# Soft-MoE attention kernel: the last batch's turns one step sooner, the last sigmoid in two parts, other PSUM places for the kept logits and the last batch's tiles

## The chip, the cores and the metric

One NeuronCore of a Trainium2 chip runs the whole program. The metric is the device time of one execution in microseconds (us). Three runs of the kernel before gave 369.21, 370.83 and 370.82 us: the median is 370.82 us.

## What is computed

Attention with a sigmoid in place of a softmax, and a soft mixture of experts on its output. Cut to what matters:

```python
B, H, S, D = 8, 12, 448, 64                      # q, k, v: float32
scores = q @ k.transpose(0, 1, 3, 2) / sqrt(D) - log(S)
x = (sigmoid(scores) @ v) -> (B * S, H * D)       # 3584 tokens x 768
logits = x @ phi                                  # 32 slots: 8 experts x 4
d = softmax(logits, over the tokens)              # dispatch
slot_out[e] = relu((d.T @ x)[e] @ w1[e]) @ w2[e]  # w1: 8 x 768 x 1024, w2: 8 x 1024 x 768
out = softmax(logits, over the slots) @ slot_out  # combine, 3584 x 768
```

## The kernel before, in words

Everything is float32. Heads are worked on in pairs: 8 batches of 6 pairs are 48 pairs. A pair's keys come in three full chunks of 128; the last 64 keys of two neighbouring pairs share a fourth. So two pairs take seven steps, `seq` has 168 of them, and a step is one `score` (L271: four products into a PSUM tile `sc`), one sigmoid over 128x896 on ScalarE (L290) and one `weigh` (L300: products with V into the `av` banks). From step 156 on a `weigh` comes one step after its `score`. `evac_a` (ScalarE) and `evac_b` (VectorE, L330) add a pair's `av` banks up into `x`. Pair 47 is cut into two parts of 256 and 192 queries in two banks (`weigh_half`, L295), with `evac_last` (L332) on VectorE.

TensorE, SyncE (SP), VectorE and ScalarE run in the order in which the code is written. **GpSimd's order alone is chosen by the scheduler** (`MANUAL`, L65, leaves it out). Waits are put in by the framework, which follows each tile as a whole: two PSUM banks that were allotted as one tile count as one.

*Turns.* The slot products need `x` with tokens on the partitions. VectorE turns it by 32x32 blocks (`turns`, L341, into a queue `todo`, which `work` empties at a pace set for each step). The last batch's turns of pairs 42 to 44 (`x` in `wpx`, turned into `wpy`) are put into the queue at steps 158 and 159 (L586, L587).

*The softmax over tokens* runs on as groups of batches end. At step 161 `slot_job` (L461) multiplies the group before the last by its weights; VectorE takes the result out of a `sc` tile (L471), which the next `score` needs. GpSimd's `old_rows` (L449) brings that sum back as rows of the last group.

*After the last step* `last_job` (L489) ends the softmax. TensorE makes the logits of pairs 45 and 46 (L497) and of 47 (L498), turns `x` of the three pairs (`turn_pe`, L356, twelve products into `px`) and does two products `warm` into `pw`, whose values nobody reads. VectorE then adds the logits and takes their maximum (L504); VectorE, GpSimd and ScalarE each move one quarter of it (L506) for a maximum over all (L507), and of the result (L509); ScalarE takes the exponentials (L512), VectorE turns them (L514), and TensorE makes the slots: `slot_mm` of `k1=1` into `pw` (L530) and of the rest into the tile of the logits (L531). VectorE turns these into `phi` (`turn_slots`, L527) and `w1` begins (L187). GpSimd also runs `old_rows` and a memset (L510, L511) for the slots of the last three pairs, which overwrite part of that `x`.

*Where things lie.* `lgt` and `pxt` are two `sc` tiles of two banks each, bank 0 and bank 1. In the kernel before bank 0 of `lgt` holds the last logits and bank 0 of `pxt` the turned pair 47; the bank 1s hold the logits of the earlier groups, copied there by `keep` (L596) for the combine softmax, since their place `ltile` is then loaded with weights (`load_kept`, L125). `pw` and `px[0]` are the `av` banks `av00` and `av01`.

*Weights.* `w1` and `w2` (50 MB) stream through a ring of tiles; SP issues all loads in the order of the code, and each waits until the tile's last reader is done. Behind the last step come loads into `big` (L169), `lt` (L127), `wpy` (which needs the products of L530 and L531 done), then three into `wa`, each for one quarter tile that the first `w1` products (L187) have read, and then whole `wa` tiles as `w1` goes on. Outputs are stored by the same queue at the end (L787, L794, L801).

## Time and profile before

| | us |
|---|---|
| median of three runs | 370.82 |
| the profiled execution, its own time | 370.77 |
| its span, from the first to the last instruction | 369.0 |
| TensorE busy (4341 matmuls) | 348.9 |
| VectorE busy | 242.5 |
| ScalarE busy | 222.3 |
| GpSimd busy | 10.1 |

The profile is of one execution; 1.77 us of its time lie outside the span. Times in the rows are us from the span's start. Attention runs to about 277.6, `last_job` to 283.9 and `w2` to 342.6; the outputs end at 369. PE is TensorE's matmuls, PEld its weight loads, DVE VectorE, ACT ScalarE, POOL GpSimd and SPq the issuing of DMAs by SP. The ends of matmuls are modelled by the profiler.

### The profile page before, as it was taken

To read this page: it belongs to the slowest core of one execution; us is meant where nothing else is said; L and a number is where in the kernel's file an instruction comes from. 1 tells how busy PE (TensorE), PEld (TensorE's weight loads), DVE (VectorE), ACT (ScalarE), POOL (GpSimd) and SP (SyncE) were. 2 spreads that over 40 slices of the span, in tenths; PEclk is the share of its full clock that TensorE was granted. 3 is DMA by queue.
4 is the path that set the end of the run, shared out by engine and by line. 5 is a ranking of instruction groups with operands and counts; after the bars stand their busy time and mean duration, and the time that the engine had idled before them with its cause. 6 is when DMAs were issued, how large, how long until landed. Compare 5 with 4: busy or idle time off the path is not lost.

```text
span 369.0 us, 10403 instructions
## 1 busy us (share of the span) xinstructions
PE 348.9 (95%) x4341; PEld 175.3 (48%) x4341; DVE 242.5 (66%) x621; ACT 222.3 (60%) x307; POOL 10.1 (3%) x45
## 2 busy tenths in 40 slices
PE   8999999999999999999999999999999999699850
PEld 5666666634444455444344644463446553233630
DVE  0158829796894986769859695978856785124650
ACT  5777777577777765777777387757573114323640
POOL 1000000000000000000000000010103001000000
PEclk9999999999999999999999999999999999979995
DMA  7666666465576663766667387739989999999998
GB/s 219 229 216 213 187 213 219 140 216 177 203 228 220 203 204 93 223 216 199 192 211 229 95 282 257 254 92 351 330 299 317 413 435 431 412 424 402 375 412 292
DMA packets 34927, 95.21 MB, mean 258 GB/s; under 512 B 3648, under 2 KB 17600, under 8 KB 33472
## 3 DMA queue, kind: packets, MB, share of 16 engines
q1 hardware_dynamic: 34880, 94.55, 72.8%
q8 instruction: 34, 0.56, 0.6%
q14 instruction: 13, 0.11, 0.1%
HBM read 83.53 MB, written 11.01 MB: 256 GB/s over the span
## 4 chain that ended last, share of the span: by engine, by line
PE 83%; DMA 8%; DVE 3%; ACT 1%; issue 1%; ACTq 0%; DVEq 0%
PE sc L281 34%; PE av L323 33%; DMA wa<-in_w_dram 7%; PE av L834 3%; PE av L187 3%; PE sc L445 2%; PE sc L383 2%; PE av L780 2%; DVE wpy L347 1%; DVE wa L781 1%; PE pt L780 1%; DMA wk<-in_qk_dram 1%; PE av L298 1%; PE av L818 1%; PE sc L365 1%; PE sc L762 1%
## 5 line engine op out<-in xcount | busy, mean ns | idle before, releaser
L290 ACT ACTIVATE big<-sc,sm 128x896 f32<-128x896 f32 x167 | 167.7, 1007 | 78.4 <-PE sc L281 75.3
L323 PE MATMUL av<-big 64*64 64x448 f32 x1292 | 163.3, 536 | 0.1
L281 PE MATMUL sc<-big 64*64 64x448 f32 x896 | 119.9, 537 | 0.4 <-DVE xy L471 0.4
L323 PEld LDWEIGHTS av<-big 64*64 64x64 f32 x1292 | 59.9, 133 | 65.3 <-issue 51.0
L281 PEld LDWEIGHTS sc<-big 64*64 64x64 f32 x896 | 42.6, 133 | 44.5 <-issue 29.3
L281 PE MATMUL sc<-wk 64*64 64x448 f32 x440 | 62.3, 538 | 0.1
L347 DVE STREAM_TRANSPOSE wa<-wpe 32x384 f32<-32x384 f32 (+5 forms) x144 | 58.0, 403 | 2.2
L347 DVE STREAM_TRANSPOSE wa<-xy 32x192 f32<-32x192 f32 (+3 forms) x96 | 33.1, 344 | 1.6
L330 DVE TENSOR_TENSOR wpe<-wpe,av 128x448 f32<-128x448 f32 x18 | 11.2, 621 | 31.5 <-PE av L323 20.3
L281 PEld LDWEIGHTS sc<-wk 64*64 64x64 f32 x440 | 21.6, 134 | 21.3 <-issue 14.5
L347 DVE STREAM_TRANSPOSE wa<-wpx 32x288 f32<-32x288 f32 (+1 forms) x48 | 24.9, 519 | 0.8
L834 PE MATMUL av<-wa,hw 128*32 128x384 f32 x208 | 21.8, 521 | 2.9 <-DMA wa<-in_w_dram 2.9
L330 DVE TENSOR_TENSOR wpx<-wpx,av 128x448 f32<-128x448 f32 x15 | 9.3, 621 | 19.8 <-PE av L323 17.5
L187 PE MATMUL av<-wa,phi 128*32 128x256 f32 x312 | 17.6, 380 | 0.4 <-DVE phi L527 0.4
L781 DVE COPY wa<-pt 128x384 f32<-128x384 f32 x23 | 11.8, 555 | 3.2 <-PE pt L780 2.8
L330 DVE TENSOR_TENSOR xy<-xy,av 128x448 f32<-128x448 f32 x14 | 8.7, 621 | 7.6 <-ACT xy L326 5.9
L781 ACT COPY wa<-av 128x384 f32<-128x384 f32 x23 | 10.6, 479 | 4.7 <-PE av L780 4.1
L187 PEld LDWEIGHTS av<-wa,phi 128*32 128x32 f32 x312 | 9.6, 110 | 7.3 <-DVE tmp L724 0.9
L727 ACT COPY t<-tmp 128x32 f32<-128x32 f32 x8 | 1.7, 218 | 17.5 <-DVE tmp L725 13.6
L771 ACT CAST big<-sc 128x512 fp32r<-128x512 f32 (+5 forms) x11 | 4.4, 432 | 11.5 <-PE sc L762 11.5
L347 DVE STREAM_TRANSPOSE wpe<-xy 32x256 f32<-32x256 f32 (+3 forms) x32 | 11.0, 344 | 0.5
L834 PEld LDWEIGHTS av<-wa,hw 128*32 128x32 f32 x208 | 5.1, 111 | 10.3 <-issue 4.7
(189 smaller groups left out, 285.0 us busy)
## 6 DMA issues: line engine op xcount, KB each, us to landing
wa<-in_w_dram SPq DMA_DIRECT2D x52, 384.0 KB, 4.0
big<-in_qk_dram SPq DMA_DIRECT2D x32, 448.0 KB, 3.6
wa<-in_wq_dram SPq DMA_DIRECT2D x6, 1536.0 KB, 30.7
wa<-in_w_dram SPq DMA_DIRECT2D x3, 3072.0 KB, 22.3
big<-in_v_dram SPq DMA_DIRECT2D x46, 192.0 KB, 2.5
wk<-in_qk_dram SPq DMA_DIRECT2D x15, 448.0 KB, 3.4
out_dram<-wa SPq DMA_DIRECT2D x13, 384.0 KB, 7.3
out_dram<-wa SPq DMA_DIRECT2D x2, 1536.0 KB, 7.4
```

Source lines behind the costliest of these rows:

```text
L187: nc.tensor.matmul(ph[32 * j:32 * j + 32, 0:256], phi_sb[:, kc, :], wt, start=(kc == 0), stop=(kc == NKC - 1))
L281: nc.tensor.matmul(sc[h][64 * t:64 * t + 64, 0:S], qkts[pt][r, S + k0:S + k0 + 64], qkts[pt][r, 0:S], start=True, stop=True)
L290: nc.scalar.activation(att, tile2[:, :, 0:S], AF.Sigmoid, bias=nbias, scale=QSCALE)
L323: nc.tensor.matmul(o[t][r, 0:S], w, att[row, h, :], start=start, stop=stop)
L330: nc.vector.tensor_tensor(out=x_of(p), in0=x_of(p), in1=av[0][:, 0:S], op=ALU.add)
L347: nc.vector.transpose(y[32 * g:32 * g + 32, k0:k0 + n, c0:c0 + m, BLK * a:BLK * a + BLK], src)
L383: nc.tensor.matmul(lg[32 * j:32 * j + 32, BLK * c0[j]:BLK * (c0[j] + n)], phi_sb[:, hp, :], blocks(x, j if x is xa else (j + 2) % 4, n), s ...
L445: nc.tensor.matmul(sls[t][32 * a:32 * a + 32, BLK * k0:BLK * k1], zt[:, c * BLK:(c + 1) * BLK], y_of(t, gi, c)[:, k0:k1, BLK * a:BLK * a + ...
L771: nc.scalar.copy(cts[i][:, m:m + w], pt[:, at0 - t0:at0 - t0 + w])
L780: nc.tensor.matmul(pf[:, 0:HALF], ct_of(m, t, n), sts[hf], start=True, stop=True)
L781: (nc.scalar.copy, nc.vector.tensor_copy)[k % 2](ov, pf[:, 0:HALF])
L834: nc.tensor.matmul(po[32 * fl:32 * fl + 32, 0:HALF], h[:, k:k + NSLOT], w2_chunk(hf, e, g, fl), start=(n == 0), stop=(n == 2 * E - 1))
```

## The change

- The last batch's turns of pairs 42 and 43 go into the queue at step 157 and are worked off there, the rest at step 158 (`LAST_T`, and a pace that begins one step sooner). `last_v` stays in step 158.
- The last sigmoid is cut into the two parts of queries (128x512 and 128x384 elements). The logits of pairs 45 and 46 stand ahead of the last product with V in TensorE's order.
- The kept logits of both halves are copied in the last step, into pair 46's banks (`av00`, `av01`). The bank 1s of `lgt` and `pxt` become `pw` and `px[0]`, and the `w1` products use them until `state["kept"]` is cleared. `load_kept` moves up by one place among the loads.

```diff
+LAST_T = 8
@@ score
+            elif u == seq[-1]:
+                flat = att.rearrange("p h s -> p (h s)")
+                att = [flat[:, 2 * t.start:2 * t.stop].rearrange("p (h s) -> p h s", h=2) for t in parts]
+                for k, t in enumerate(parts):
+                    nc.scalar.activation(att[k], tile2[:, :, t], AF.Sigmoid, bias=nbias, scale=QSCALE)
@@ last_job
             evac_last(p)
-            logits(lg, b, range(TR, NPR - 1), first=TR)
@@ the table of steps
-        late[u + SLOT_AT] += [lambda: turns(B - 1, 0, 0, 2, 0, EARLY), lambda: work(B * S)]
-        late[u + SLOT_AT + 1] = [lambda: turns(B - 1, 0, 2, 1, 0, EARLY), lambda: turns(B - 1, 0, 0, 3, EARLY)]
+        del late[u + SLOT_AT]
+        late[u + LAST_T] = [lambda: work(B * S), lambda: turns(B - 1, 0, 0, 2, 0, EARLY), lambda: work(B * S)]
+        late[u + LAST_T + 1] = [lambda: turns(B - 1, 0, 2, 1, 0, EARLY), lambda: turns(B - 1, 0, 0, 3, EARLY)]
-        for i in range(u + 10, u + 31):
+        for i in range(u + 9, u + 31):
@@ keep
-            nc.vector.tensor_copy(t[:, 1, 0:w], lts[i][:, 0:w])
+            nc.vector.tensor_copy(t[:, 0:w], lts[i][:, 0:w])
@@ the loop over the steps
                 if i == len(seq) - 1:
+                    kept = [ps_av.tile([P, 512], F32, name=f"av0{t}") for t in range(2)]
+                    keep(1, kept[1])
                     lgt = ps_sc.tile([P, 2, 512], F32, name="sc")
-                    keep(1, lgt)
+                    keep(0, kept[0])
                     logits_old(lgt[:, 0, :])
             else:
-                nc.scalar.activation(dmx[0:1, :], atts[seq[-1]][0:1, 0, 0:1], AF.Exp)
+                logits(lgt[:, 0, 0:P], B - 1, range(TR, NPR - 1), first=TR)
+                nc.scalar.activation(dmx[0:1, :], atts[seq[-1]][1][0:1, 0, 0:1], AF.Exp)
@@ after the loop
-        pw = ps_av.tile([P, 512], F32, name="av00")
-        px = [ps_av.tile([P, 512], F32, name="av01")]
         pxt = ps_sc.tile([P, 2, 512], F32, name="sc")
-        keep(0, pxt)
-        px += [pxt[:, 0, :], ps_av.tile([P, 512], F32, name="av10")]
+        pw, px = lgt[:, 1, :], [pxt[:, 1, :], pxt[:, 0, :], ps_av.tile([P, 512], F32, name="av10")]
@@ av_tile
+        if name == "av0" and state["kept"]:
+            return (lgt, pxt)[turn[name] % 2][:, 1, :]
...
-        if k == 6:
+        if k == 5:
             load_kept()
```

How it moves instructions, at three places. Engines' waits stand in brackets.

VectorE at steps 157 to 161, before: L330 adds up pair 44, L347 are the turns, L471 takes the slots out of their `sc` tile.

```order
L330 TENSOR_TENSOR wpx_72<-wpx_72,av00_2788 128x448 [waits PE_49,Activation_49]
L347 STREAM_TRANSPOSE wpy_73<-wpx_72 32x2x4x32 [waits DVE_49]
L347 STREAM_TRANSPOSE wpy_73<-wpx_72 32x2x4x32 x5
L347 STREAM_TRANSPOSE wpy_73<-wpx_72 32x4x32 [waits DVE_49]
L347 STREAM_TRANSPOSE wpy_73<-wpx_72 32x4x32 x5
L347 STREAM_TRANSPOSE wpy_73<-wpx_72 32x3x4x32 x2
L476 MEMSET t1_2660 64x32
L471 SCALAR_TENSOR_TENSOR xy_89<-xy_89,t1_2660,sc_2878 128x3x32 [waits PE_49]
L471 SCALAR_TENSOR_TENSOR xy_89<-xy_89,t1_2660,sc_2878 128x3x32
L347 STREAM_TRANSPOSE wpy_73<-wpx_72 32x3x3x32 x8
```

The same place now (L337, L354 and L478 are what L330, L347 and L471 were):

```order
L354 STREAM_TRANSPOSE wpy_73<-wpx_72 32x2x4x32 [waits DVE_49]
L354 STREAM_TRANSPOSE wpy_73<-wpx_72 32x2x4x32 x5
L337 TENSOR_TENSOR wpx_72<-wpx_72,av00_2788 128x448 [waits PE_49,Activation_49]
L354 STREAM_TRANSPOSE wpy_73<-wpx_72 32x4x32 [waits DVE_49]
L354 STREAM_TRANSPOSE wpy_73<-wpx_72 32x4x32 x5
L354 STREAM_TRANSPOSE wpy_73<-wpx_72 32x3x4x32 x2
L354 STREAM_TRANSPOSE wpy_73<-wpx_72 32x3x3x32 x3
L483 MEMSET t1_2660 64x32
L478 SCALAR_TENSOR_TENSOR xy_89<-xy_89,t1_2660,sc_2881 128x3x32 [waits PE_49]
L478 SCALAR_TENSOR_TENSOR xy_89<-xy_89,t1_2660,sc_2881 128x3x32
L354 STREAM_TRANSPOSE wpy_73<-wpx_72 32x3x3x32 x5
```

Six turns moved ahead of the addition, and three more ahead of the row that empties the slots' tile.

GpSimd (POOL) after the last step, before: the copies to `sm` are its quarters of the maximum, those to `xy` are `old_rows`.

```order
L451 COPY xy<-xy 32x3x32 [waits DVE_49,Pool_49]
L506 COPY sm<-sm 32x1 [waits DVE_49]
L509 COPY sm<-sm 32x1 [waits DVE_49]
L451 COPY xy<-xy 32x3x32 [waits PE_49]
L451 COPY xy<-xy 32x3x32
L511 MEMSET xy 32x3x128 [waits Pool_49]
```

And now:

```order
L458 COPY xy<-xy 32x3x32 [waits DVE_49,PE_49]
L458 COPY xy<-xy 32x3x32
L517 MEMSET xy 32x3x128 [waits Pool_49]
L512 COPY sm<-sm 32x1 [waits DVE_49]
L515 COPY sm<-sm 32x1 [waits DVE_49]
```

The two copies of `old_rows`, which wait for TensorE's last turn of `x`, and the memset moved ahead of the quarters of the maximum.

TensorE over the same stretch, before: L298 is the end of the last product with V, L365 the logits, L359 the turns, L339 `warm`, L445 the slots; a buffer's number tells its tile.

```order
L298 MATMUL av11_2981<-big_75,xy_89 64x192 x2
L365 MATMUL sc_3005<-xy_89,phi_69 32x96 [waits DVE_49,PE_49]
...
L365 MATMUL sc_3005<-xy_89,phi_69 32x64 [waits DVE_49]
...
L365 MATMUL sc_3005<-xy_89,phi_69 32x32 x2
L359 MATMUL av01_3021<-csb_66,xy_89 128x128 x3
...
L359 MATMUL av10_3024<-csb_66,xy_89 64x128
L339 MATMUL av00_3020<-csb_66 128x128 x2
L445 MATMUL av00_3020<-wpy_73,t1_2660 32x32 [waits DVE_49]
L445 MATMUL av00_3020<-wpy_73,t1_2660 32x32 x11
L445 MATMUL av00_3020<-wpy_73,t1_2660 32x32 [waits Pool_49] x4
L445 MATMUL sc_3005<-wpy_73,t1_2660 32x64 x16
```

And now (L305, L372, L366, L346 and L452 are what L298, L365, L359, L339 and L445 were):

```order
L372 MATMUL sc_3009<-xy_89,phi_69 32x128 x2
L305 MATMUL av10_2980<-big_75,xy_89 64x256 [waits Activation_49]
L305 MATMUL av10_2980<-big_75,xy_89 64x256
L305 MATMUL av11_2981<-big_75,xy_89 64x192 [waits Activation_49]
L305 MATMUL av11_2981<-big_75,xy_89 64x192
L372 MATMUL sc_3009<-xy_89,phi_69 32x64 [waits DVE_49]
...
L366 MATMUL av10_3033<-csb_66,xy_89 64x128
L346 MATMUL sc_3009<-csb_66 128x128 x2
L452 MATMUL sc_3009<-wpy_73,t1_2660 32x32 [waits DVE_49]
L452 MATMUL sc_3009<-wpy_73,t1_2660 32x32 x11
L452 MATMUL sc_3009<-wpy_73,t1_2660 32x32 [waits Pool_49] x4
L452 MATMUL sc_3009<-wpy_73,t1_2660 32x64 x16
```

The logits of two pairs moved ahead of the last V, and `warm` and the first slots, which went to a bank of their own (`av00_3020`), now go to the tile that holds the logits (`sc_3009`).

VectorE's readers of these tiles, before:

```order
L504 ISA t1_2660,sm_67<-sc_3005,t1_2660 128x128 [waits DVE_49,PE_49]
...
L527 STREAM_TRANSPOSE phi_69<-av00_3020 128x32 [waits DMAHW6_49,PE_49]
L485 COPY xy_89<-av01_3021 128x128 [waits Activation_49]
L527 STREAM_TRANSPOSE phi_69<-sc_3005 128x64 [waits PE_49]
L487 COPY xy_89<-sc_3022 64x128 [waits Pool_49]
L487 COPY xy_89<-av10_3024 64x128
```

And now:

```order
L510 ISA t1_2660,sm_67<-sc_3009,t1_2660 128x128 [waits DVE_49,PE_49]
...
L533 STREAM_TRANSPOSE phi_69<-sc_3009 128x32 [waits DMAHW6_49,PE_49]
L492 COPY xy_89<-sc_3032 128x128 [waits Activation_49]
L533 STREAM_TRANSPOSE phi_69<-sc_3009 128x64
L494 COPY xy_89<-sc_3032 64x128
L494 COPY xy_89<-av10_3033 64x128
```

The rows stand in the same order and read other tiles. Of the two turns of the slots only the first still waits for TensorE. In the built program the count for which L504 waited was that of the last logits' product; L510's is that of the second `warm` product. The count for the first turn of the slots (L527, now L533) was that of the last 32x32 product and is now that of the last 32x64 product.

## Rows read from the trace of the kernel before

**Rows 1.** Busy time by stretch: window, length, engines, granted clock, DMA share, GB/s

```profile
280.00:285.00 5.00, 4.50 (x143) 2.99 (x146) 3.20 (x14) 1.44 (x7) 2.02 (x7) 1.00 0.86 310
285.00:290.00 5.00, 5.00 (x91) 2.93 (x87) 3.50 (x14) 0.45 (x2) 0.85 (x4) 1.00 1.03 390
```

**Rows 2.** Chain of waits in time order: start, us, what

```profile
287.02 7.95 PE av L187 x144
294.99 27.03 DMA wa<-in_w_dram
322.06 1.51 PE av L834 x8
```

**Rows 3.** Timeline of SP's issues: start, us, queue, line, DMA

```profile
281.45 0.33 SPq L169 DMA_DIRECT2D wpy<-in_w_dram  x1
282.04 1.78 SPq L165 DMA_DIRECT2D wa<-in_wq_dram  x3
285.47 1.62 SPq L169 DMA_DIRECT2D wa<-in_wq_dram  x2
```

**Rows 4.** Timeline at steps 158 to 162: start, us, engine, line [idle before <-releaser]

```profile
259.55 0.62 DVE L330 TENSOR_TENSOR wpx<-wpx,av 128x448 f32<-128x448 f32 x1 [1.79 <-PE av L323]
...
266.53 3.86 DVE L347 STREAM_TRANSPOSE wpy<-wpx 32x288 f32<-32x288 f32 x8
...
266.64 0.98 PE L281 MATMUL sc<-big 64*64 64x448 f32 x8 [0.41 <-DVE xy L471]
```

**Rows 5.** Timeline, end of attention

```profile
274.80 0.53 DVE L598 COPY sc<-lt 128x352 f32<-128x352 f32 x1 [1.20 <-ACT big L290]
...
275.59 1.01 ACT L290 ACTIVATE big<-sc,sm 128x896 f32<-128x896 f32 x1 [0.82 <-PE sc L281]
...
276.65 0.98 PE L298 MATMUL av<-big,xy 128*64 128x256 f32 x8 [0.28 <-ACT big L290]
...
277.56 0.87 PE L365 MATMUL sc<-xy,phi 128*32 128x96 f32 x32
```

**Rows 6.** Timeline, from the maximum to the first products with w1

```profile
278.51 0.29 DVE L504 CUSTOM_DVE_ANT_0 t<-sc,t 128x128 f32<-128x128 f32 x1 [0.45 <-PE sc L365]
...
278.87 0.18 POOL L506 COPY sm<-sm 32x1 f32<-32x1 f32 x1 [11.01 <-DVE sm L504]
...
279.18 0.14 DVE L507 TENSOR_REDUCE sm<-sm 32x1 f32<-32x4 f32 x1 [0.19 <-ACT sm L506]
279.29 0.60 PE L359 MATMUL av<-csb,xy 128*128 128x128 f32 x4
...
279.72 0.61 PE L339 MATMUL av<-csb 128*128 128x128 f32 x4
...
279.95 0.56 POOL L451 COPY xy<-xy 32x96 f32<-32x96 f32 x2 [0.38 <-PE av L359]
...
280.43 0.46 PE L445 MATMUL av<-wpy,t 128*32 128x32 f32 x32
...
280.57 0.41 POOL L511 MEMSET xy<- 32x384 f32 x1
...
280.70 0.68 PE L445 MATMUL sc<-wpy,t 128*32 128x64 f32 x32
...
281.07 0.22 DVE L527 STREAM_TRANSPOSE phi<-av 128x32 f32<-128x32 f32 x1 [0.18 <-PE av L445]
...
281.34 1.50 PE L187 MATMUL av<-wa,phi 128*32 128x256 f32 x24
281.42 0.25 DVE L527 STREAM_TRANSPOSE phi<-sc 128x64 f32<-128x64 f32 x1
```

**Rows 7.** Busy time by half us where TensorE last stood still

```profile
319.00:319.50 0.50, 0.34 (x3) 0.10 (x1) 0.32 (x2) 0.06 (x1) 0.00 (x0) 1.00 0.87 369
...
321.00:321.50 0.50, 0.00 (x0) 0.00 (x0) 0.00 (x0) 0.00 (x0) 0.00 (x0) 0.92 0.99 393
...
328.00:328.50 0.50, 0.50 (x5) 0.15 (x3) 0.00 (x0) 0.00 (x0) 0.00 (x0) 0.76 0.99 418
```

More of the change, by code (lines that the diff above doesn't have):

```diff
@@ L97, in soft_moe_attention @@
     N_SEQ = len(units) - 2
-    state = {"next": 0, "ring": 0, "used": 0, "room": 0, "n8": 0, "call": 0}
+    state = {"next": 0, "ring": 0, "used": 0, "room": 0, "n8": 0, "call": 0, "kept": True}
     utile, quads = {}, {}
@@ L296, in weigh_half @@
             for k, t in enumerate(parts):
+                a = att[k] if isinstance(att, list) else att[:, :, t]
                 for h, r in enumerate(heads):
-                    nc.tensor.matmul(o[k][r, 0:t.stop - t.start], w[:, r], att[:, h, t], start=start, stop=stop)
+                    nc.tensor.matmul(o[k][r, 0:t.stop - t.start], w[:, r], a[:, h, :], start=start, stop=stop)
         def weigh(u):
@@ L597, in keep @@
             n, w = 0, LTW[i]
-            nc.vector.tensor_copy(t[:, 1, 0:w], lts[i][:, 0:w])
+            nc.vector.tensor_copy(t[:, 0:w], lts[i][:, 0:w])
             for gi in range(2 * i, 2 * i + 2 + i):
                 wd = (lt_at + [lt_at[-1]])[gi].shape[1]
-                lt_ps[gi] = t[:, 1, n:n + wd]
+                lt_ps[gi] = t[:, n:n + wd]
                 n += wd
@@ L624, in last_v @@
         def last_v():
-            assert not todo and state["next"] == N_1 + N_X
+            assert state["next"] == N_1 + N_X
             for p in (NP - 2, NP - 1):
@@ L628, in last_v @@
             load(1)
-        late[(B - 1) * per_b + LAG + SLOT_AT].insert(1, last_v)
+        late[(B - 1) * per_b + LAG + LAST_T + 1].insert(0, last_v)
         done = 0
@@ L868, in soft_moe_attention @@
                 sctx.close()
+                state["kept"] = False
                 ps_t = ctx.enter_context(tc.tile_pool(name="ps_t", bufs=4, space=PSUM, reuse_waits="tile"))
```

## The prediction

> **What bounds the kernel now.** I read the busy time by stretch first, then the chain of waits, then the timelines of the engines and of SP's issues around the end of attention. The reader is to see that the bound changes hands there. In 280 to 285 the transfer engines are busy 0.86 of the time, and in the next stretch 1.03 [rows 1], that is, without a gap. The chain then holds TensorE until 294.99, and a load of 27.03 us, after which TensorE goes on at 322.06 [rows 2]: TensorE has caught up with the weights and waits for them. So the end follows the moment at which the unbroken stream of weights begins. That stream begins with the load into `wpy`, issued at 281.45, and three loads into `wa` from 282.04 [rows 3]; the first waits for the slots' products L445, the others for the first products with `w1`, L187. TensorE's own delay would cost little by itself. What costs or gives time is when these four loads are let go, and the chain from the last batch to L187 at 281.34 is what I cost.
>
> **The turns, one step sooner.** VectorE stood still for 1.79 us ahead of the addition of pair 44 [rows 4]. The six turns that now stand there take at most 6 x 0.48 = 2.9 us (0.48 is 3.86/8, the length of the larger turns [rows 4]). They fill the gap, and the addition comes up to 1.1 us later, which nobody notices: the logits that read it come two steps behind it. Behind it VectorE is 1.79 us ahead, but three more of the larger turns now stand ahead of L471: 1.79 - 3 x 0.48 = 0.35 us, of which I take 0.30, for the handover between turns and addition. The next `score` waits 0.41 us for L471 [rows 4], so it takes the whole 0.30; bounds 0 and 0.41. The last turns end about 1.8 us sooner, and so do the loads into `wpx` behind them; the transfers ahead of the gap in 275 to 277 end sooner, and the gap grows. What is late next is `wpy`, so these loads give the end nothing, and neither does `load_kept`, one place further up.
>
> **The sigmoid in two parts, and the logits ahead of the last V.** TensorE stands still for 0.28 us ahead of the last V, waiting for the sigmoid of 1.01 us [rows 5]. The logits of two pairs are half of the 32 passes of 0.87 us, some 0.35 to 0.44 us [rows 5]; they fill the 0.28 and the first part of the sigmoid (about 0.6 us, by size) is done by then. So the last V starts and ends within 0.1 us of where it did. The logits of pair 47 still wait for VectorE's `evac_last` behind V's second part, which set their end before; I take 0.05 us gained, bounds -0.1 and 0.2. [...] The copies of the kept logits now stand where VectorE waited 1.20 us [rows 5]; without that gap they would cost up to their 0.53 + 0.63 us in `evac_last`.
>
> **The new banks: two waits.** Here I read the order and the built waits against the timeline. Until now the maximum L504 followed the last logits at once: they ended at 277.56 + 0.87 = 278.43, it began at 278.51 [rows 5, 6]. TensorE's twelve turns (end 279.29 + 0.60 = 279.89) and `warm` (end 279.72 + 0.61 = 280.33) ran beside VectorE's chain [rows 6]. Now `warm` writes into bank 1 of the tile whose bank 0 holds the logits, and L504 waits for `warm`. With 0.35 us gained above, `warm` ends at 279.98, and the maximum begins at 280.07 (with the same lag): **1.56 us later** than in the trace.
>
> On GpSimd the two copies of `old_rows` and the memset now stand ahead of its quarters of the maximum. The copies wait for TensorE's last turn, at 279.89 - 0.35 = 279.54. Before, from 279.95 to 280.57 + 0.41 = 280.98 these three took 1.03 us [rows 6]. So GpSimd is free at 279.60 + 1.03 = 280.63, and its quarter of 0.18 us ends near 280.85. The other engines' quarters take from 278.51 to 279.09 before (0.09 ahead of L507 at 279.18), 0.58 us, which gives 280.65 now. GpSimd is last by 0.20, and L507 begins at 280.95: **1.77 us later**, bounds 1.4 (`warm` signals sooner than its modelled end, and GpSimd is hidden) and 2.1 (nothing of the first two parts is gained).
>
> That GpSimd cannot take the quarter past the waiting copy is shown by no row alone: in the trace it stood still 0.38 us ahead of these copies with only their followers behind it [rows 6]. The Trainium skill (TensorE: Matmul & The Clock Gate, section Architectural detail: the array is 16× 32×32, not 1× 128×128) calls GpSimd's queue a strict first-in first-out one; by it the sum holds as it stands. If the quarter could go ahead, the delay would be 1.56 instead of 1.77.
>
> From L507 to the slots nothing changes, so L445 begins at 280.43 + 1.77 = 282.20, and its second group ends at 281.38 + 1.77 = 283.15, which lets `wpy` go **1.8 us later**, at 283.25. Both groups are now in one tile, and the first turn of the slots waits for the second group too: before it began at 281.07, now it can begin where the second one did, at 281.42 [rows 6], 0.35 us later still. L187 thus begins at 281.34 + 1.77 + 0.35 = 283.46, and the three `wa` loads go **2.1 us later**.
>
> **The sum.** The stream starts 1.8 us later with `wpy`, and its saturation with `wa` 2.1 us later, but in the 0.3 us between them `wpy` still flows. I take 1.9 us, nearer to the first, bounds 1.4 and 2.3. Behind it the transfer engines have no gap in which to make this up, so it goes to the end: 370.77 + 1.9 = 372.67 for the profiled execution, which stands 0.05 under the median of the runs: 372.7 us.
>
> **The rivals.**
>
> *The clock falls too (slower still).* TensorE now stands still from 279.98 to 282.20, for 2.2 us. In the trace it stopped at 319.34; the granted clock was 1.0 until about 321.42 (0.92 as the mean of that half us), then 0.5, which is 1.2 for 2.4 GHz, until about 328.24 (0.76) [rows 7]: a halt of 2.1 us came before that fall, and 6.8 us at half. For it: the new halt is as long. Against: the engine was at work at full clock for long ahead of it, and short halts (0.41 us) brought no fall. The price: in 6.8 us at half, 3.4 us of work are lost. `wpy` and the three `wa` loads together keep the transfer engines busy for some 6 us (by their shapes, 128x1536 and three of 128x1024 floats, 2304 KB, at 390 GB/s [rows 1]), while the next load comes 4.0 us behind `wpy`'s [rows 3] and would come at 7.4: a new gap of about 1.4 to 2.2 us. That gives 374.4 us. The same page of the Trainium skill, section What's actually happening, says that the throttled state is the default and activity releases it; by it 374.4 becomes likelier, but no row shows how near this halt is.
>
> *The delay is taken up by the stream (not slower).* TensorE waits from 319.34 to 322.06 for weights, 2.7 us, more than its delay of 2.1. If the transfer engines could bring the same bytes faster, because they were limited by when loads were let go and not by their rate, the load that TensorE awaits would land when it did, and the end would be where it was, or 0.3 us ahead: 370.5 us. It decides from 1.9 us of room in the stream between 285 and 322. Against it stands the busy share of 1.03 at 390 GB/s [rows 1].
>
> *The change does only what it says.* If neither wait binds (the maximum begins behind the logits, GpSimd's quarter is in time), L187 is 0.35 us sooner: 370.4 us. The order and the built waits speak against it.
>
> **How the numbers follow.** Forecast 0.56, clock 0.24, taken up 0.12, only what it says 0.08. The predicted time is the forecast's, 372.7 us. The bounds of its own terms are 372.2 and 373.1. The range goes up to the clock's case with its upper price and down to short of the two faster ones: 370.9 to 374.7. About 0.5%, or 1.85 us, is what a measurement of this kernel can tell from no change, so slower begins at 372.67, in the midst of my forecast. Slower: 0.30 of the 0.56 and 0.23 of the 0.24, 0.53. Faster by as much, under 368.97, is open only if the sooner loads of `wpx` and `ltile` (1.8 us and more) counted for the end in the last two cases: 0.05. Same: 0.42.
>
> **What would show it.** Right: L471's follower `score` waits about 0.1 us; the maximum begins near 280.1, at the end of `warm`; GpSimd's copies of `old_rows` stand at 279.6 and the next reduction waits for its quarter, near 281; `wpy` goes at 283.2 and L187 begins at 283.5; the share of the transfers in 280 to 285 is well under 0.86, and everything from 322 on is shifted by one amount. Wrong: a maximum that begins at 278.2; transfers with gaps behind 287, or a landing at 322 as before; a granted clock of 0.5 near 284, which is the clock's rival.

## The result, and the profile after

The changed kernel took **373.04 us** (median of 6 runs, 372.19 to 373.53) beside 370.51 us of the kernel before (6 runs): 1.0073 times as long, 95% interval 1.0052 to 1.0094. The profiled execution took 372.19 us, the shortest of the six, with a span of 370.4 us.

VectorE at the turns of the last batch, TensorE's next score, and the loads behind the last turn (timeline: start, us, engine, line, operation, [idle before <-releaser]):

```profile
260.48 0.62 DVE L337 TENSOR_TENSOR wpx<-wpx,av 128x448 f32<-128x448 f32 x1
...
265.70 0.54 DVE L478 SCALAR_TENSOR_TENSOR xy<-xy,t,sc 128x96 f32<-128x96 f32 x2
...
266.39 0.98 PE L282 MATMUL sc<-big 64*64 64x448 f32 x8 [0.16 <-PE av L330]
...
268.72 0.80 SPq L170 DMA_DIRECT2D wpx<-in_w_dram  x2
```

The addition L337 begins 0.93 us later than its row in [rows 4], the score 0.25 us sooner (266.39 for 266.64), and its wait is 0.16 instead of 0.41 us. The loads into `wpx` go at 268.72.

From the last sigmoid to the first products with `w1`, in the same view:

```profile
276.05 0.64 PE L372 MATMUL sc<-xy,phi 128*32 128x96 f32 x16
...
276.62 0.98 PE L305 MATMUL av<-big,xy 128*64 128x256 f32 x8
277.35 0.69 DVE L342 COPY xy<-av 128x256 f32<-128x256 f32 x2 [1.94 <-PE av L305]
...
277.83 0.57 PE L372 MATMUL sc<-xy,phi 128*32 128x64 f32 x16 [0.23 <-DVE xy L342]
...
279.69 0.61 PE L346 MATMUL sc<-csb 128*128 128x128 f32 x4
...
279.92 0.56 POOL L458 COPY xy<-xy 32x96 f32<-32x96 f32 x2 [12.31 <-PE av L366]
280.34 0.29 DVE L510 CUSTOM_DVE_ANT_0 t<-sc,t 128x128 f32<-128x128 f32 x1 [2.30 <-PE sc L346]
280.53 0.41 POOL L517 MEMSET xy<- 32x384 f32 x1
...
281.00 0.18 POOL L512 COPY sm<-sm 32x1 f32<-32x1 f32 x1
281.21 0.14 DVE L513 TENSOR_REDUCE sm<-sm 32x1 f32<-32x4 f32 x1 [0.40 <-POOL sm L512]
...
282.47 0.95 PE L452 MATMUL sc<-wpy,t 128*32 128x32 f32 x64 [2.16 <-DVE t L520]
...
283.72 1.50 PE L188 MATMUL av<-wa,phi 128*32 128x256 f32 x24 [0.31 <-DVE phi L533]
```

The maximum L510 has waited 2.30 us, not for the logits (they end at 278.40) but for a product of L346, which is `warm` and ends by the profiler's model at 280.30. GpSimd's quarter L512 begins when `old_rows` and the memset are done, and L513 waits 0.40 us for it alone. TensorE stands still for 2.16 us ahead of the slots. Against [rows 6] the maximum is 1.83 us later, L513 2.03, the slots 2.04, the first products with `w1` 2.38.

SP's issues; the chain of waits (start, us, what); TensorE's two waits for weights behind 318; and the busy time by stretch (window, length, engines, granted clock, DMA share, GB/s), all of the changed kernel:

```profile
283.48 0.33 SPq L170 DMA_DIRECT2D wpy<-in_w_dram  x1
284.42 1.32 SPq L166 DMA_DIRECT2D wa<-in_wq_dram  x3
```

```profile
308.89 33.23 DMA wpe<-in_wq_dram
```

```profile
323.50 1.51 PE L843 MATMUL av<-wa,hw 128*32 128x384 f32 x8 [2.23 <-DMA wa<-in_w_dram]
...
342.26 0.85 PE L843 MATMUL av<-wpe,hw 128*32 128x384 f32 x8 [0.92 <-DMA wpe<-in_wq_dram]
```

```profile
280.00:285.00 5.00, 2.53 (x91) 1.70 (x93) 3.17 (x16) 2.05 (x8) 1.21 (x5) 1.00 0.48 165
285.00:290.00 5.00, 4.59 (x100) 2.80 (x94) 2.71 (x10) 0.26 (x1) 1.76 (x6) 1.00 0.93 322
```

Against [rows 3] `wpy` goes 2.03 us later and the `wa` loads 2.38. The transfers' share fell to 0.48 in 280 to 285 and to 0.93 in the next stretch, for 0.86 and 1.03 in [rows 1], and the clock stayed at 1.00. The load that TensorE awaited until 322.06 [rows 2] now lets it go on at 323.50, 1.44 us later: less than the 2.03 and 2.38 us by which the loads were let go later. Before, TensorE did not wait for weights again behind 322.06. Now it waits once more, 0.92 us for the last weights (`wpe`), and the chain goes over that load instead. In this execution the span grew by 1.4 us.

### The profile page after: what moved, and what is told of

Its sections match the earlier page's. It is cut to its first block, busy times and chain, and to the rows that moved or that the text cites. A ratio compares the mean times of both kernels' runs of the same rounds, so it can differ in the third digit from the quotient of the medians.

```text
span 370.4 us, 10406 instructions
## 1 busy us (share of the span) xinstructions
PE 348.0 (94%) x4341; PEld 159.4 (43%) x4341; DVE 242.5 (65%) x621; ACT 223.4 (60%) x308; POOL 10.1 (3%) x45
## 4 chain that ended last, share of the span: by engine, by line
PE 84%; DMA 9%; DVE 2%; ACT 1%; issue 0%; POOL 0%; ACTq 0%
PE sc L282 35%; PE av L330 33%; DMA wpe<-in_wq_dram 9%; PE sc L188 5%; PE sc L452 3%; PE sc L390 2%; DVE wa L790 1%; PE av L843 1%; PE av L789 1%; PE sc L372 1%; PE av L188 1%; PE av L568 1%; PE av L305 1%; PE pt L789 1%; PE sc L366 0%
## 5 line engine op out<-in xcount | busy, mean ns | idle before, releaser
L330 PE MATMUL av<-big 64*64 64x448 f32 x1292 | 150.4, 536 | 0.0
L282 PE MATMUL sc<-big 64*64 64x448 f32 x896 | 111.8, 537 | 0.2 <-PE av L330 0.2
L330 PEld LDWEIGHTS av<-big 64*64 64x64 f32 x1292 | 48.7, 133 | 73.1 <-issue 70.3
L354 DVE STREAM_TRANSPOSE wa<-wpe 32x384 f32<-32x384 f32 (+5 forms) x144 | 58.0, 403 | 2.2
L282 PE MATMUL sc<-wk 64*64 64x448 f32 x440 | 59.5, 548 | 0.0
L282 PEld LDWEIGHTS sc<-big 64*64 64x64 f32 x896 | 35.6, 133 | 49.9 <-issue 40.0
L354 DVE STREAM_TRANSPOSE wa<-xy 32x192 f32<-32x192 f32 (+3 forms) x96 | 33.1, 345 | 1.6
L337 DVE TENSOR_TENSOR wpe<-wpe,av 128x448 f32<-128x448 f32 x18 | 11.2, 621 | 31.7 <-PE av L330 20.4
L282 PEld LDWEIGHTS sc<-wk 64*64 64x64 f32 x440 | 18.5, 136 | 23.8 <-issue 19.7
L354 DVE STREAM_TRANSPOSE wa<-wpx 32x288 f32<-32x288 f32 (+1 forms) x48 | 25.0, 520 | 0.8
L843 PE MATMUL av<-wa,hw 128*32 128x384 f32 x208 | 20.9, 507 | 2.2 <-DMA wa<-in_w_dram 2.2
L337 DVE TENSOR_TENSOR wpx<-wpx,av 128x448 f32<-128x448 f32 x15 | 9.3, 621 | 17.9 <-PE av L330 15.6
L188 PE MATMUL sc<-wa,phi 128*32 128x256 f32 x264 | 14.7, 380 | 0.0
L337 DVE TENSOR_TENSOR xy<-xy,av 128x448 f32<-128x448 f32 x14 | 8.7, 621 | 9.1 <-ACT xy L333 7.4
L354 DVE STREAM_TRANSPOSE wpe<-xy 32x256 f32<-32x256 f32 (+3 forms) x32 | 11.0, 344 | 0.5
L188 PEld LDWEIGHTS sc<-wa,phi 128*32 128x32 f32 x264 | 8.4, 110 | 5.7 <-DVE tmp L733 0.6
L354 DVE STREAM_TRANSPOSE wpy<-wpx 32x288 f32<-32x288 f32 (+3 forms) x22 | 9.3, 423 | 0.4
```

Of the source, the lines that this page charges most:

```text
L188: nc.tensor.matmul(ph[32 * j:32 * j + 32, 0:256], phi_sb[:, kc, :], wt, start=(kc == 0), stop=(kc == NKC - 1))
L282: nc.tensor.matmul(sc[h][64 * t:64 * t + 64, 0:S], qkts[pt][r, S + k0:S + k0 + 64], qkts[pt][r, 0:S], start=True, stop=True)
L330: nc.tensor.matmul(o[t][r, 0:S], w, att[row, h, :], start=start, stop=stop)
L337: nc.vector.tensor_tensor(out=x_of(p), in0=x_of(p), in1=av[0][:, 0:S], op=ALU.add)
L354: nc.vector.transpose(y[32 * g:32 * g + 32, k0:k0 + n, c0:c0 + m, BLK * a:BLK * a + BLK], src)
L843: nc.tensor.matmul(po[32 * fl:32 * fl + 32, 0:HALF], h[:, k:k + NSLOT], w2_chunk(hf, e, g, fl), start=(n == 0), stop=(n == 2 * E - 1))
```

## The experiments

My theory: two new waits (VectorE's for `warm`, and its wait for GpSimd's quarter) let the loads go later, and the transfers cannot make it up. Rivals: another part of the change costs the time; the pause of TensorE costs it, by the clock or as TensorE's own delay. Positions in the program shift by up to 1 us between executions, so I count from VectorE's first copy out of the last V (`evac_last`): before it began at 277.38 (the line below) and `wpy` went 4.07 us behind it, the `wa` loads 4.66; in the changed kernel 6.13 and 7.07. Ratios are to the kernel before, with 95% intervals.

```profile
277.38 0.69 DVE L335 COPY xy<-av 128x256 f32<-128x256 f32 x2
```

**`warm` in a tile of its own.**

```diff
-            warm(pw, 2)
+            ph0 = ps_av.tile([P, 512], F32, name="av11")
+            warm(ph0, 2)
```

> One edit on the changed kernel: the two filler passes `warm` write into the tile of ph0 (av11) instead of bank 1 of the tile that holds the logits. With that the order of GpSimd goes back too: its quarters stand ahead of two of the three `old_rows` copies again. Theory of the two waits (mine): the maximum no longer follows `warm` at 280.34 us, but the last logits, near 278.5; the next reduction begins near 279.2 instead of 281.21, the slots near 280.4 instead of 282.47, `wpy` goes near 281.5 instead of 283.48, and the first three `wa` loads near 282.4 instead of 284.42, still some 0.35 later than before because the first turn of the slots waits for both groups. All of the loss but some 0.2 us is gone: about 370.7 us. Theory of the other parts (the sooner turns, the split sigmoid or the moved logits cost the time): the maximum moves, the end stays near 373.0. Theory of the halt (TensorE's pause of 2.16 us costs by itself): also near 370.7, but then a TensorE that is late behind the loads costs as much.

Measured: 370.90 us, ratio 1.0005 (0.9993 to 1.0017). Its timeline:

```profile
277.49 0.69 DVE L342 COPY xy<-av 128x256 f32<-128x256 f32 x2 [1.94 <-PE av L305]
...
278.62 0.29 DVE L511 CUSTOM_DVE_ANT_0 t<-sc,t 128x128 f32<-128x128 f32 x1 [0.44 <-PE sc L372]
...
279.29 0.14 DVE L514 TENSOR_REDUCE sm<-sm 32x1 f32<-32x4 f32 x1 [0.19 <-ACT sm L513]
...
281.56 0.33 SPq L170 DMA_DIRECT2D wpy<-in_w_dram  x1
...
282.50 0.69 SPq L166 DMA_DIRECT2D wa<-in_wq_dram  x1
```

With `warm` in another tile the loss is gone. The maximum follows the logits' product again, GpSimd, whose order goes back with this edit, is in time again, and `wpy` goes 4.07 us behind the copy, as before. The `wa` loads are 0.35 us late (5.01 behind it), which is the wait of the first slot turn for the second group; it leaves no trace in the time. The theory of the other parts falls: they all still stand in this kernel.

**The same wait put into the kernel before.**

```diff
-            warm(pw, 2)
+            warm(lgt[:, 0, P:2 * P], 2)
```

> One edit on the kernel before: `warm` writes into the tile of the logits, columns 128 to 256 of their own bank, and nothing else of the change is made; slots, kept logits, turns and sigmoid stay where they were. GpSimd's order changes as in the changed kernel. Theory of the two waits: the maximum begins at 280.38 (where `warm` ends) instead of 278.51, GpSimd ends its quarter near 281.2, so the reduction is 2.0 us later, near 281.2, `wpy` goes near 283.5 and the `wa` loads near 284.0, and the end is 2.0 us later: about 372.5 us. Theory of the other parts: no more than 0.3 us, 370.5 to 370.8.

Measured: 372.91 us, ratio 1.0055 (1.0037 to 1.0073). Its timeline:

```profile
277.45 0.69 DVE L335 COPY xy<-av 128x256 f32<-128x256 f32 x2
...
280.45 0.29 DVE L504 CUSTOM_DVE_ANT_0 t<-sc,t 128x128 f32<-128x128 f32 x1 [2.31 <-PE sc L339]
...
281.11 0.18 POOL L506 COPY sm<-sm 32x1 f32<-32x1 f32 x1
281.32 0.15 DVE L507 TENSOR_REDUCE sm<-sm 32x1 f32<-32x4 f32 x1 [0.40 <-POOL sm L506]
...
283.59 0.33 SPq L169 DMA_DIRECT2D wpy<-in_w_dram  x1
...
284.18 0.80 SPq L165 DMA_DIRECT2D wa<-in_wq_dram  x2
```

Here `warm` writes other columns than the logits, 128 to 256 of their bank, and VectorE waits for it all the same; in the changed kernel it writes another bank of the same tile, and VectorE waits too. So the wait follows neither columns nor banks but the tile. With no other edit the slowdown is there, and both kinds of loads go 2.07 us later. GpSimd's order changes with the edit, as in the changed kernel.

**GpSimd's quarter on VectorE.**

```diff
-            for j, copy in ((1, dve), (2, pool), (3, act)):
+            for j, copy in ((1, dve), (2, dve), (3, act)):
                 copy(m1[0:32, j:j + 1], m1[32 * j:32 * j + 32, 0:1])
```

> One edit on the changed kernel: the quarter of the maximum that GpSimd copied behind `old_rows` and its memset is copied by VectorE. The wait for `warm` stays. Theory of the two waits: the maximum stays at 280.3, the next reduction begins near 281.0 instead of 281.21 (0.2 us, the part of GpSimd that sticks out beyond `warm`, less a second copy of about 0.1 us on VectorE), loads 0.1 to 0.2 sooner, about 372.8 us. If GpSimd's order were the main cause and `warm` only ran beside it, the reduction would begin at 279 to 280 and the end would be near 371.

Measured: 372.99 us, ratio 1.0057 (1.0040 to 1.0075). Its timeline:

```profile
277.70 0.69 DVE L342 COPY xy<-av 128x256 f32<-128x256 f32 x2 [1.94 <-PE av L305]
...
280.69 0.29 DVE L510 CUSTOM_DVE_ANT_0 t<-sc,t 128x128 f32<-128x128 f32 x1 [2.31 <-PE sc L346]
...
281.43 0.14 DVE L513 TENSOR_REDUCE sm<-sm 32x1 f32<-32x4 f32 x1
...
283.70 0.33 SPq L170 DMA_DIRECT2D wpy<-in_w_dram  x1
```

From the maximum to the reduction it is 0.74 us instead of 0.87, and `wpy` goes 6.00 us behind the copy instead of 6.13. Taking this quarter off GpSimd gives 0.13 us. The wait for `warm` is most of the delay: in the changed kernel the maximum begins 2.99 us behind the copy instead of 1.13, 1.86 of the 2.06 us by which `wpy` is late.

**The parts alone, on the kernel before.** First the turns: `LAST_T = 8`, with the calls of `turns`, the place of `last_v` and the start of the faster rate as in the change.

> On the kernel before only the first part of the change: the last batch's turns a step sooner, with the place of the last V's loads that goes with it. Theory of the two waits: TensorE's score behind the turns is 0.25 us sooner, as in the trace of the changed kernel, and so is all behind it up to `wpy` (281.2) and `wa` (281.8): 370.2 to 370.5 us. Theory that this part costs the time of the change: 372 to 373 us.

Measured: 370.31 us, ratio 0.9990 (0.9974 to 1.0007). Then the sigmoid in two parts and the logits of two pairs ahead of the last V, with banks and turns as they were.

> On the kernel before only the second part: the last sigmoid in two parts and the logits of pairs 45 and 46 ahead of the last V; banks, kept logits and turns stay. In the trace of the changed kernel the last V was 0.2 us late against the score ahead of it, so I expect it at 276.85 instead of 276.65, the maximum near 278.7 instead of 278.51, and the loads 0.2 us later: 370.7 to 371.0 us. Theory that this part costs the time: 372 to 373 us. As I had predicted it (a gain of 0.05 us): 370.6 us.

Measured: 370.63 us, ratio 0.9998 (0.9985 to 1.0010). The timelines of the turns alone and then of the second part alone, from the score behind the turns:

```profile
266.60 0.98 PE L282 MATMUL sc<-big 64*64 64x448 f32 x8 [0.16 <-PE av L324]
...
277.33 0.69 DVE L336 COPY xy<-av 128x256 f32<-128x256 f32 x2
```

```profile
267.30 0.98 PE L281 MATMUL sc<-big 64*64 64x448 f32 x8 [0.42 <-DVE xy L477]
...
276.95 0.64 PE L371 MATMUL sc<-xy,phi 128*32 128x96 f32 x16
...
278.25 0.69 DVE L341 COPY xy<-av 128x256 f32<-128x256 f32 x2 [0.19 <-PE av L304]
```

The turns shorten the score's wait, from 0.41 us [rows 4] to 0.16. From that score to the copy out of the last V it is 10.73 us, and 10.74 before; with the second part it is 10.95: the logits ahead of V cost 0.21 us. So one part gives 0.25 and the other takes it, and neither can be told from no change in the time. Turns alone are, with `warm` and the slot in tiles of their own (below), the shortest versions I found, and neither is measurably faster than the kernel before.

**TensorE late, once behind the loads and once ahead.** Both kernels are the one before with seven more filler passes, about 1.8 us.

```diff
             w1_mm(ph0, 0, range(TR))
+            warm(pw, 7)
```

> One edit on the kernel before: seven more filler passes of 128x128 on TensorE behind the first products with `w1`, so that TensorE is about 1.5 to 2 us later from 283 on, while `wpy` and the first three `wa` loads go when they did (281.45 and 282.04); the next two `wa` loads go later by the filler, about 287. Theory of the stream (the moment at which these loads go sets the end): TensorE caught up anyway and waited 2.7 us for weights near 320; no change, 370.2 to 370.8 us. Theory that TensorE's own delay goes to the end: 372.0 to 372.5 us.

Measured: 370.88 us, ratio 1.0005 (0.9990 to 1.0020).

```diff
-            warm(pw, 2)
+            warm(pw, 9)
```

> One edit on the kernel before: the same seven filler passes as in the run with a late TensorE, but ahead of the slots' products instead of behind the first products with `w1`: `warm` makes nine passes instead of two. VectorE's maximum and GpSimd stay as they were. Seven passes took 1.83 us there; the last of the two ends at 280.33 in the kernel before, so the slots begin at about 281.9 instead of 280.43, `wpy` goes near 282.95 and the `wa` loads near 283.55, each 1.5 us later. Theory of the stream: the end is 1.5 us later, 372.2 us, although the same filler behind the loads cost 0.2 us at most. Theory that it is the wait of VectorE or GpSimd that costs, by something other than when the loads go: no change, 370.7 us.

Measured: 371.30 us, ratio 1.0021 (1.0008 to 1.0033), some 0.8 us (0.3 to 1.2). The timelines, first with the filler behind the loads:

```profile
278.33 0.69 DVE L335 COPY xy<-av 128x256 f32<-128x256 f32 x2
...
282.40 0.33 SPq L169 DMA_DIRECT2D wpy<-in_w_dram  x1
...
283.73 1.83 PE L339 MATMUL av<-csb 128*128 128x128 f32 x14
```

```profile
277.90 0.69 DVE L335 COPY xy<-av 128x256 f32<-128x256 f32 x2
...
280.25 2.17 PE L339 MATMUL av<-csb 128*128 128x128 f32 x18
...
283.37 0.33 SPq L169 DMA_DIRECT2D wpy<-in_w_dram  x1
```

Behind the loads the filler costs nothing measurable, though it takes TensorE 1.8 us and lets the next two `wa` loads go 1.9 us later against the copy: TensorE's own delay is not the price. Ahead of them it lets `wpy` go 1.40 us later (5.47 behind the copy), and the end moves, but by about half of that. The 1.5 us that I had expected were wrong, and with it the rule that a delay of the loads goes to the end one to one.

What fits somewhat better is how long the transfer engines stood idle. The busy time by stretch, for the 14 us behind the copy out of the last V, in the kernel before, in the one with the filler ahead, and in the changed one (the last two columns are the share and GB/s):

```profile
277.38:291.38 14.00, 13.50 (x306) 9.15 (x306) 9.66 (x39) 3.58 (x14) 3.27 (x12) 1.00 0.96 356
```

```profile
277.90:291.90 14.00, 13.60 (x292) 9.84 (x292) 8.33 (x35) 3.37 (x13) 3.27 (x12) 1.00 0.91 331
```

```profile
277.35:291.35 14.00, 10.89 (x246) 7.32 (x246) 7.73 (x31) 3.27 (x13) 3.15 (x12) 1.00 0.80 286
```

The idle time, 14 us times what is missing from 1, is 0.56, 1.26 and 2.80 us. All kernels in this view, against two effects. One is read in the same profiled execution: by how much later than before, counted from the copy, TensorE goes on with the load that it awaits near 322 (44.68 us behind the copy before). The other is the time lost over all runs:

| kernel | share | idle more than before, us | `wpy` / `wa` behind the copy, us | awaited load later, us | ratio to before, in us of 370.6 |
|---|---|---|---|---|---|
| before | 0.96 | 0 | 4.07 / 4.66 | 0 | 0 |
| turns alone | 0.99 | -0.42 | 4.07 / 4.66 | -1.34 | -0.4 |
| sigmoid and logits alone | 0.95 | 0.14 | 4.07 / 4.66 | -0.49 | -0.1 |
| `warm` in its own tile | 0.94 | 0.28 | 4.07 / 5.01 | -0.07 | 0.2 |
| that, and the first slots in it too | 0.94 | 0.28 | 4.06 / 4.86 | -0.11 | -0.2 |
| filler behind the loads | 0.95 | 0.14 | 4.07 / 4.67 | 0.19 | 0.2 |
| filler ahead of the loads | 0.91 | 0.70 | 5.47 / 6.06 | -0.03 | 0.8 |
| before with `warm` in the logits' tile, two profiles | 0.88, 0.88 | 1.12, 1.12 | 6.14 / 6.73, 6.13 / 6.73 | 0.59, 0.71 | 2.0, 1.7 |
| quarter off GpSimd | 0.80 | 2.24 | 6.00 / 6.94 | 1.44 | 2.1 |
| changed kernel, three profiles | 0.80, 0.82, 0.81 | 2.24, 1.96, 2.10 | 6.13 / 7.07 in each | 1.47, 1.39, 1.40 | 2.7, 2.4, 3.2 |
| changed kernel, pause filled | 0.81 | 2.10 | 6.14 / 7.08 | 1.26 | 1.7 |

The awaited load follows the idle time: 0.6 to 0.7 us later where the gap is 1.12 us larger, 1.3 to 1.5 where it is 2.0 to 2.2 larger. The release of `wpy` does not order it: in these two groups of kernels `wpy` goes equally late. Up to a gap of 0.7 us the executions scatter by more than the effect. The time over all runs fits less well: with `warm` in the logits' tile the kernel before lost 1.7 to 2.0 us on a gap of 1.12, the changed kernel with its pause filled 1.7 on 2.10. In all kernels with a gap of 0.7 us or more it grew by more than the awaited load was late; the traces do not show where. A part may lie ahead of the copy: the other two profiled executions of the changed kernel took 372.74 and 372.76 us instead of 372.19, and their copy begins at 278.05 and 278.11 instead of 277.35.

With the same release of `wpy`, the changed kernel leaves twice the extra gap of the kernel before with `warm` in the logits' tile. Its loads ahead of the gap had gone sooner (`wpx` at 268.72, in the other at 270.49), and its transfer engines ran dry sooner: in the fifth, sixth and seventh us behind the copy their share is 0.53, 0.02 and 0.00, in the other kernel 0.90, 0.46 and 0.13. Its `wa` loads also go 0.34 us later, which alone is less than the 0.7 to 0.9 us between the awaited loads of the two. The shares have two digits, so each idle time is good to 0.07 us.

**`warm` and the first slots in their own tile.** The first edit, and besides it:

```diff
-            sls = [pw[:, 0:BLK], lg[:, 0:SLN // 2], pw[:, SLN // 2:SLN]]
+            sls = [ph0[:, 512 - BLK:512], lg[:, 0:SLN // 2], pw[:, SLN // 2:SLN]]
```

> The kernel of the run with `warm` in its own tile, and besides it the first group of the slots' products also goes into the tile of ph0 (columns 480 to 512), so that the first turn no longer waits for the second group. Theory of the two waits: that turn begins near 281.15 instead of 281.53, the first products with `w1` near 281.45 instead of 281.80, the three `wa` loads near 282.15 instead of 282.50; `wpy` stays near 281.56. The end follows by 0.1 to 0.35 us: 370.5 to 370.8 us against 370.9, which a measurement hardly tells apart; the rows decide. Theory that only `wpy` counts: 370.9 us.

Measured: 370.40 us, ratio 0.9994 (0.9982 to 1.0007). The `wa` loads go 4.86 us behind the copy instead of 5.01: 0.15 of the 0.35 us; the turn now begins right behind VectorE's copies L492 that stand ahead of it. The time cannot be told from that of the kernel before.

**Does the pause cost by itself?** The changed kernel and the two others with a TensorE at rest lost 1.7 to 3.2 us, more than their gap in some runs. So I filled the pause and ran the changed kernel again beside it.

```diff
             warm(pw, 2)
+            ph0 = ps_av.tile([P, 512], F32, name="av11")
+            warm(ph0, 7)
```

> One edit on the changed kernel: behind `warm`, seven more filler passes of 128x128 on TensorE, into the tile of ph0, which nobody waits for before the slots' products. They took 1.83 us in the other runs and so fill most of the pause of 2.16 us ahead of the slots. Both new waits stay, and so do the times at which the loads go (`wpy` 283.5, `wa` 284.4). Where the same delay of the loads came from a busy TensorE (nine passes ahead of the slots), loads 1.4 us late cost 0.8 us; where it came with a TensorE at rest (the changed kernel and the two others with `warm` in the logits' tile), loads 2.0 us late cost 2.0 to 2.5 us. Theory that the pause itself costs, by a lower clock in some executions behind it: the end comes some 0.7 to 1 us sooner than that of the changed kernel, 371.6 to 372.3 us, and its slowest executions are gone. Theory that only the moment of the loads counts: no change, 373.0 us.

> The changed kernel once more, beside the one with its pause filled, for a comparison on the same chip and a second look at TensorE's clock behind the pause of 2.16 us. Theory of the loads alone: 373.0 us, with the granted clock at 1.0 from 280 to 290 as in the first profile. Theory that the pause itself costs: executions in two groups, about 372.2 to 372.8 and 373.3 to 373.5 us, and, if the profile is of the second, a fall of the clock near 284.

Measured: 372.42 us with the pause filled, ratio 1.0046 (1.0029 to 1.0062); 372.74 us for the changed kernel, ratio 1.0066 (1.0042 to 1.0089). The intervals overlap. With the pause filled TensorE stands still for only 0.60 us ahead of the slots, and 1.7 us are lost all the same: these are not the pause's. Over all of its runs in this study the changed kernel has a mean of 373.1 (18 executions, standard error 0.16), the filled one 372.4 (10 executions, 0.17): a hint of 0.7 us, no proof. Both kernels with the pause were then profiled again, for the clock.

> The changed kernel a third time, for the clock of one more execution. So far: with its pause at rest 372.19 to 374.45 us in 13 executions (mean 373.0), with the pause filled 371.42 to 373.35 in 10 (mean 372.4). Theory that the pause costs by the clock: a profiled execution of over 373 us with a clock below 1.0 between 282 and 290. Theory of the loads alone: the clock at 1.0 there in this one too, whatever its time, and the start of the `wpy` and `wa` loads against the last V at 6.9 and 7.8 us as in the two others.

> The kernel before with `warm` in the logits' tile once more, for the same reason: its executions so far lie at 371.39 to 371.66 (two), 372.3 to 372.69 (two) and 373.12 to 373.47 us (four), and the profiled one was the fastest, with the clock at 1.0 from 280 to 355. Theory that the pause costs by the clock: an execution of over 373 us shows a clock below 1.0 between 282 and 290. Theory of the loads alone: a time near 372.5, the clock at 1.0 there, and what differs between executions lies elsewhere, ahead of the last V or in the rate of the transfers behind 290.

Measured: 373.48 us, ratio 1.0087 (1.0066 to 1.0109), and 372.17 us, ratio 1.0047 (1.0019 to 1.0076). Busy time by stretch of the changed kernel in this profile, the third column from the right being the clock:

```profile
280.00:285.00 5.00, 2.53 (x86) 2.00 (x88) 2.64 (x14) 2.04 (x8) 1.28 (x5) 1.00 0.55 201
285.00:290.00 5.00, 4.60 (x102) 2.77 (x94) 2.76 (x10) 0.26 (x1) 1.76 (x6) 1.00 0.89 315
```

In all six profiled executions with this pause (three of the changed kernel, two of the kernel before with `warm` in the logits' tile, one with the quarter off GpSimd) the clock is 1.00 from 280 to 290. It falls later in some, as here behind 323 (0.77 as the mean of 325 to 330). But the profiled ones took 371.39 to 372.76 us, and none of those above 373 was profiled. So that the clock falls near 284 was never seen, and what makes some executions longer than 373 us is open.

## Why the prediction was right, point by point

- **What bounds the kernel.** Right: the transfers behind the last batch, not TensorE. A TensorE late by 1.8 us behind the loads cost nothing measurable, the same filler ahead of them did. In twelve of the fourteen profiled executions TensorE also waited for the last weights, near 341; only in those of the kernel before and of `warm` in its own tile did it not wait again behind 322.
- **The turns.** The addition came 0.93 us later (at most 1.1 was named), the score 0.25 us sooner (0.30), its wait fell to 0.16.
- **The logits ahead of the last V.** This is the term that was mis-sized. I gave the logits of two pairs 0.35 to 0.44 us, half of a run of 32 passes. From their start (276.05) to that of the last V (276.62) it took 0.57 us: the run of 16 lasts 0.64 us by itself, where all 32 in one run lasted 0.87 [rows 5]. Only 0.28 us of standing still was there to be filled, so the last V came later, which took back the 0.25 us that the turns gave, as the part alone shows (0.21), so the logits ended at 278.40 instead of 278.08, and every step behind was about 0.26 us later than I put it: the maximum at 280.34 for 280.07, L513 at 281.21 for 280.95, the slots at 282.47 for 282.20, `wpy` at 283.48 for 283.25, L188 at 283.72 for 283.46. The sigmoid did not hold the last V up: its two parts end at 276.50 (1.16 us from 275.34, where the undivided one took 1.01 [rows 5]).
- **The two waits.** Right in mechanism and order: the maximum began 0.04 us behind `warm`'s modelled end, removing this wait (with the order of GpSimd that goes with it) removes the loss, and adding it to the kernel before brings a loss. GpSimd added 0.20 us from the maximum to the reduction (0.87 for 0.67), as forecast, of which 0.13 can be had back. Whether GpSimd could take the quarter past a waiting instruction stays open: the quarter's value was there at 280.64, when the memset had already begun (280.53), so the quarter could not have gone ahead of it in any case. It began at 281.00, behind the memset. The Trainium skill (TensorE: Matmul & The Clock Gate, section Architectural detail: the array is 16× 32×32, not 1× 128×128) has GpSimd take its queue strictly in order; no row here shows it. The prediction's other case, a delay of 1.56 us, was not open: by its own times, too, the memset would have begun near 280.22 and the maximum ended at 280.36.
- **The sum.** 1.9 us were forecast, 2.5 measured (1.9 to 3.5 from the interval); 372.7 and 373.04 us. The forecast was worked out for the profiled execution, and there two errors met. The loads went 2.03 and 2.38 us later instead of 1.8 and 2.1, by the mis-sized term. But "no gap in which to make this up" was wrong: the awaited load was only 1.44 us later, and the execution took 372.19 us, 1.42 more than before. So some 0.6 us of the delay was taken up before 322. That 372.7 lies between this execution and the median of the runs is partly luck: why the other runs of the changed kernel took longer is not known.
- **The signs.** "Everything from 322 on is shifted by one amount" came out only roughly: 1.44 us at the awaited load, 1.21 at the first products behind the last weights (343.19 and 344.40), 1.4 at the end, with a new wait of 0.92 us between.
- **The rivals.** The clock did not fall at 284 in any profiled execution. The stream took up a part of the delay, not all of it: some 0.6 us in the changed kernel, about 1.4 of 2.07 us in the kernel before with `warm` in the logits' tile, and, ahead of the loads, all of the filler's 1.40 us in the profiled execution, about half of it by the time over all runs. That the change does only what it says was excluded by the row of the maximum.

## What to carry to other kernels

A wait follows the tile, not the bank and not the columns: before filler or any idle-time work is pointed at a free part of a tile, look at who reads that tile next. Where a stream of loads sets the end, look at how long the transfer engines stand idle, and not only at how late a load goes: here the idle time ordered the arrival of the awaited weights, though not all of the time lost. And half of a run of small products can cost more than half of its time, as it did here (0.57 of 0.87 us).

## What the runs showed of the hardware

How long TensorE stood still did not tell whether its clock fell. Waiting for weights near 320 it stood still for 2.61 us with the sigmoid and logits alone and kept its clock, and for 1.82 us in the second profile of the kernel before with `warm` in the logits' tile, and lost it (for each TensorE's timeline, then the busy time by stretch with the clock third from the right):

```profile
322.44 0.85 PE L840 MATMUL av<-wa,hw 128*32 128x384 f32 x8 [2.61 <-DMA wa<-in_w_dram]
```

```profile
325.00:330.00 5.00, 5.00 (x48) 1.78 (x40) 1.42 (x3) 1.78 (x5) 0.42 (x2) 1.00 1.01 425
```

```profile
322.99 1.34 PE L834 MATMUL av<-wa,hw 128*32 128x384 f32 x8 [1.82 <-DMA wa<-in_w_dram]
```

```profile
325.00:330.00 5.00, 5.00 (x36) 2.17 (x34) 1.12 (x2) 1.13 (x3) 0.21 (x1) 0.84 1.01 425
```

Where it fell, it went to half (0.5, which is 1.2 GHz), for 6.8 us in the kernel before [rows 7] and for 3.4 us in the first profile of the changed kernel. The Trainium skill (TensorE: Matmul & The Clock Gate, section What's actually happening) has activity release a throttle that is the default; that a pause can bring it back agrees with these rows, but the pause's length alone did not decide it here. Nor did the end follow the clock. The profiled execution of `warm` in its own tile had 0.66 and 0.65 in 320 to 325 and 325 to 330 and took 370.58 us; that of the sigmoid and logits alone had 1.00 in both and took 371.23. At full clock TensorE came to the later weights before they were there: it waited for three more loads (0.27, 0.98 and 1.04 us), the last one until 341.26. At half clock it had no such wait behind 322.10.

```profile
341.26 0.85 PE L840 MATMUL av<-wpe,hw 128*32 128x384 f32 x8 [1.04 <-DMA wpe<-in_wq_dram]
```
